# Pacing the last weight conversion, giving the block sums buffers of their own, and dropping a scan buffer in a fused recurrence and two-MLP kernel

## The chip, the cores and the metric

The kernel runs on one core of one Trainium2 chip, alone. The metric is the device time of one execution in microseconds (us); less is better. A profiled execution gives, beside its time, the span from the first to the last instruction.

## The reference

A linear recurrence over 768 steps on 32 heads (4 batches, 8 heads of size 40) is followed by two MLPs over its 3072 tokens of width 320. Everything comes in as float64 words for the MLP weights and float32 for the rest; the output is float32.

```python
for t in range(S):                       # the recurrence, per head
    y[:, :, t] = einsum('bhd,bhde->bhe', rt, state)
    Sa = einsum('bhde,bhe->bhd', state, at)
    state = state * wt[:, :, None, :] - einsum('bhd,bhe->bhde', Sa, bt) + einsum('bhd,bhe->bhde', vt, kt)
...
h = x @ w_in                             # first MLP, 320 -> 2048 -> 320
x = (maximum(h, 0) + alpha * minimum(h, 0)) @ w_out
...
g = x @ w_gate                           # second MLP, 320 -> 1536 -> 320
out = (g * (1 / (1 + exp(-g))) * (x @ w_val)) @ w_out
```

## The kernel before, in words

**Stages.** The tokens are cut into six pieces m of 128 steps by four batches, 512 columns each. For each piece the recurrence is done in chunk form (`preps`, `inverse`, `seq`), its result goes to DRAM as `xd[m]`, and the first MLP takes that piece as its block j = m (`mlp1`), one piece behind the recurrence, so that blocks 0 to 3 and the start of block 4 run beside the recurrence of the next piece. When the recurrence has ended, its memory pools are closed, and the tail begins: the rest of block 4, block 5 (the last), and then the six blocks of the second MLP.

**Numbers in two halves.** Each float32 operand of a product is split into a high part (an ACT cast, `split`, L198) and the rest (a subtraction, L199), and products are made of high and low parts: 8 matmuls for an up product (`up_mm`, L254) and 8 for a down product (`down_mm`, L260 to L266). Weights come as float64, are turned into float32 by integer work on VectorE, an ACT operation and, for every other tile, two on GpSimd (`gated`, L186 to L194), are split, and are kept in DRAM (`wd`) or, for the last tiles, in memory.

**A block of the first MLP.** For each of 16 tiles f of the hidden width: fetch the up weights (`fetch`, L244), up product into `u`, `prelu` (an ACT relu L294, a VectorE operation L295, the split into `gh` and `gl`), and one step behind it the down product, which adds into three sums `d`. Blocks 0 to 4 fetch into a ring of four weight buffers (pool `wp1`, tag `w`); from tile 10 of block 4 on, tiles are fetched into buffers that block 5 uses again ("resident"). At the end of a block the three sums are copied out (L356, L359, L360) and written to DRAM as `x1d[j]` (L357, L361). Their copies `x1o` stand in the two buffers of tag `g`, which `prelu` uses too. `fill_x` loads and splits the x of a block; for `mlp1` it is traced at a priority raised by 1000.

**Order.** Nothing here waits by hand. A scheduler orders each engine's instructions before the run: of those whose operands and buffers are free by its own reckoning it takes the one with the best priority, which is the place in the traced program, raised where the code says so. `tc.issue_after(x)` puts those instructions of its block that stand on x's own engine behind x in that engine's order. A pool that is opened where closed pools lay waits for the last use of each closed pool that it overlaps.

**The tail's other work.** `direct` converts tiles 4 to 11 of the three weight matrices of the second MLP (24 tiles; gate, value and out in turn) straight into memory; `kept` fetches tiles 0 to 3, converted earlier. During block 5, one tile of `direct` is traced at every `CTAIL`-th step; the rest is traced in the first block of the second MLP, three tiles per f. The x of that first block, `xs0`, is traced right behind the x of block 5. In the second MLP, per f: gate product `pg`, value product `pv` (two buffers each), a Silu on ACT (`sg`, L986), a product, a split, and the down products (L972 to L974). The pool `gp` with `sg` is opened when the pools of the first MLP are closed.

**The scan of `prep_a`.** Each item (a batch of a piece) has a scan of the decays (L525) into `rest`, of which two exist; from it come `Wx` (L532) and `AN` (L539) in `prep_a`, and `kbt` in `prep_b` (L552). `preps` traces `kbt` of an item ahead of the scan of the next.

Of the kernel before, what the change touches and what calls it, by code (L numbers as in the profile page):

```python
# [7 lines left out]
F32 = mybir.dt.float32  # L8
F32R = mybir.dt.float32r
U32 = mybir.dt.uint32  # L10
# [8 lines left out]
XPRI = 1000  # L19
# [20 lines left out]
ZB = 2  # L40
# [7 lines left out]
YB = 1  # L48
# [10 lines left out]
GPB = 2  # L59
DEP = 1  # L60
HOLD = 10
CTAIL = 8
XB = 2
L = 64
HALF = 32
LOOK = 2
AHEAD = 3
KEEP = 4

@with_exitstack  # L70
def kernel(
# [15 lines left out]
    nc = tc.nc  # L87
    NM, B, _, D, NP, TB = r.shape
    NT, DM = out.shape
# [3 lines left out]
    NSEG = NP * CPB  # L93
    NG = B * NSEG
    BLK = B * TB
    NB = NT // BLK
    K1 = DFF // 128
    K2 = DFF2 // 128
    RT = DM - 256
    lo, hi = slice(0, 64), slice(64, 128)  # L100
# [4 lines left out]
    x1d = [dram.tile([DM, BLK], F32, name=f"x1d{m}") for m in range(NM)]  # L105
# [49 lines left out]
    mark = {}  # L155

    @contextmanager
    def lifted():
        tc.cur_priority -= XPRI
        yield  # L160
        tc.cur_priority += XPRI

    def words(x):
        return x.bitcast(U32).rearrange("f (n two) -> f n two", two=2)
# [13 lines left out]
    LEAST = 1.125 * 2.0 ** -15  # L178

    def gated(pool, raw, dve=0):  # L180
        whi, wlo = raw[..., 1], raw[..., 0]
        sh = list(whi.shape)
        y = pool.tile(sh, U32, tag="wy", name="wy", bufs=YB)
        z = pool.tile(sh, U32, tag="wz", name="wz", bufs=ZB)
        f = z.bitcast(F32)
        nc.vector.tensor_scalar(y, whi, 0x07FFFFFF, 3, ALU.bitwise_and, ALU.logical_shift_left)  # L186
        nc.vector.scalar_tensor_tensor(z, whi, 0xC0000000, y, ALU.bitwise_and, ALU.bitwise_or)
        nc.vector.scalar_tensor_tensor(y, wlo, 29, z, ALU.logical_shift_right, ALU.bitwise_or)
        nc.scalar.activation(out=f, in_=whi.bitcast(F32), func=ACTF.Abs)
        if dve:  # L190
            nc.vector.scalar_tensor_tensor(f, f, LEAST, y.bitcast(F32), ALU.is_ge, ALU.mult)
            return f
        nc.gpsimd.tensor_scalar(f, f, LEAST, None, ALU.is_ge)
        nc.gpsimd.tensor_tensor(out=f, in0=f, in1=y.bitcast(F32), op=ALU.mult)  # L194
        return f

    def split(raw, h, l, eng):
        nc.scalar.copy(out=h, in_=raw)  # L198
        eng.tensor_tensor(out=l, in0=raw, in1=h.bitcast(F32), op=ALU.subtract)  # L199
# [87 lines left out]
    def load_x(pool, src, n):  # L287
        xs = new_x(pool, n)
        fill_x(pool, xs, src, 0, n)
        return xs  # L290

    def prelu(gpool, ps, f, n):
        g = gpool.tile([128, n], F32, tag="g", name="g")
        nc.scalar.activation(out=g, in_=ps, func=ACTF.Relu, scale=-1.0)  # L294
        nc.vector.scalar_tensor_tensor(g, g, neg[:, f:f + 1], ps, ALU.mult, ALU.add)  # L295
        gh = gpool.tile([128, n], F32R, tag="gh", name="gh")
        gl = gpool.tile([128, n], F32R, tag="gl", name="gl")
        split(g, gh, gl, nc.gpsimd if f % 16 < PGL else nc.vector)
        return gh, gl
# [18 lines left out]
    def mlp1(j, early=0):  # L318
        psd, xp1, gp1, wp1 = (e1p[k] for k in ("psd", "xp", "gp", "wp"))
        fs = [*range(HOLD, K1), *range(HOLD)] if j == NM - 1 else range(K1)  # L320
        half = B // 2 * TB
        xs = new_x(xp1, BLK)
        plan = [(f, 0, half) for f in range(early)] + [(f, half, BLK) for f in range(early)]
        plan += [(f, 0, BLK) for f in fs if f >= early]
        dps = [psd.tile([128, BLK], F32, tag=f"d{q}", name=f"d{q}") for q in range(3)]
        pend = []
        done = ups

        def down(f, c0, c1, gh, gl):
            t = fetch(wp1, 2 * f + 1, False, j, done)  # L330
            for q in range(3):
                down_mm(dps[q][:, c0:c1], q, t, gh, gl, f == fs[0] and c0 == 0, f == fs[-1])

        seen = set()
        for f, c0, c1 in plan:
            if not seen & {(c0, c1), (0, half) if early and c0 == 0 else (c0, c1)}:
                with lifted():
                    b0, b1 = c0 // TB, c1 // TB
                    fill_x(xp1, xs, xd[j][:, b0:b1].rearrange("f b t -> f (b t)"), c0, c1)
                seen.add((c0, c1))  # L340
                yield
            t = fetch(wp1, 2 * f, True, j, done)
            ps = e1p["psu"].tile([128, c1 - c0], F32, tag="u", name="u")
            done.append(up_mm(ps, t, tuple(x[..., c0:c1] for x in xs)))
            yield
            if len(pend) == DEP:
                down(*pend.pop(0))
            pend.append((f, c0, c1, *prelu(gp1, ps, f, c1 - c0)))
            yield
        for e in pend:  # L350
            down(*e)
        for q in range(3):
            tc.cur_priority -= XPRI
            o = gp1.tile([128, BLK], F32, tag="g", name="x1o")
            if q < 2:
                nc.scalar.copy(out=o, in_=dps[q])  # L356
                nc.sync.dma_start(out=x1d[j][q * 128:q * 128 + 128], in_=o)  # L357
            else:
                nc.scalar.copy(out=o[lo], in_=dps[2][hi])  # L359
                nc.vector.tensor_tensor(out=o[lo], in0=dps[2][lo], in1=o[lo], op=ALU.add)  # L360
                mark["x1"] = nc.sync.dma_start(out=x1d[j][256:DM], in_=o[lo])  # L361
            tc.cur_priority += XPRI
            yield
# [21 lines left out]
    nc.gpsimd.memset(first, 0.0)  # L385
    reset = first[:, 0:NSEG // 2]
    nc.gpsimd.memset(reset[:, :, 0:1], 1.0)
    rests = [rawp.tile([128, NSEG, L + 1], F32, name=f"rest{j}") for j in range(2)]
    mask = pers.tile([128, L], F32, name="mask")

    def masks():
# [526 lines left out]
    wg, wv2, w2 = {}, {}, {}  # L918
    KINDS = ((wg, moe2_w_gate, "up"), (wv2, moe2_w_val, "up"), (w2, moe2_w_out, "down2"))

    def direct():
        for f in range(KEEP, K2):
            for j, (held, src, kind) in enumerate(KINDS):
                t = wpool.tile([128, 768 if kind == "up" else 2 * DM], F32R, tag=f"w{j}", name=f"w{j}")
                conv(tail, 2 * K1 + 3 * f + j, src, f, kind, t, (3 * f + j) % 2)
                held[f] = t.rearrange("p (a b) -> p a b", a=6) if kind == "up" else t
                yield

    def kept(f):
        for j, (held, _, kind) in enumerate(KINDS):  # L930
# [6 lines left out]
    with ExitStack() as st:  # L937
        e1p["psu"] = st.enter_context(tc.tile_pool(name="psu3", bufs=3, space=PSUM))
        for _ in gm:
            pass  # L940
        XAB[0] = 4
        gm = mlp1(NM - 1)
        next(gm)
        xs0 = load_x(xp, x1d[0], BLK)
        for k, _ in enumerate(gm):
            if k % CTAIL == 2:
                next(c2, 0)
        last1 = fetched[-2 * HOLD:]
        for f in range(KEEP):
            with tc.issue_after(last1[LOOK + 4 * f].ins):  # L950
                kept(f)
# [100 lines left out]
```

## Time and profile before

| | us |
|---|---|
| median of 3 runs (1256.48 to 1261.86) | 1259.91 |
| the profiled execution's own time | 1257.29 |
| its span | 1255.3 |
| outside the span | 2.0 |
| TensorE (PE) busy in the span | 1100.4 |
| VectorE (DVE) busy | 754.6 |
| ScalarE (ACT) busy | 605.0 |
| GpSimd (POOL) busy | 282.0 |

Times in rows are us from the start of the span, lengths of single instructions in us unless marked ns. PE is TensorE's matmuls, PEld its weight loads, SPq the queue of SyncE, which issues nearly all transfers. A bracket behind a row gives the time that the engine sat idle before it and what ended it. "Clock" is the granted clock of TensorE as a share of 2.4 GHz. The profiled execution lies 2.6 us under the median.

### The profile page before, as it was taken

What the parts mean: (1) busy time and instruction counts of PE and PEld (TensorE: products, weight loads), DVE (VectorE), ACT (ScalarE), POOL (GpSimd) and SP (SyncE); (2) the same over time, 40 slices, a digit from 0 to 9 for tenths busy, and PEclk for the clock granted to TensorE, in tenths of its full rate; (3) what the DMA queues carried; (4) which work ended last, traced back from release to release, by engine and by line L of the source; (5) the groups of instructions that cost most, each with busy time, mean ns of one, the idle gap of its engine ahead of it and who ended that gap; (6) DMA issues with size and microseconds to landing.
All of it is one profiled execution on the core that took longest, in us unless ns stands there. A gap on an engine that the chain in (4) does not pass through costs nothing.

```text
span 1255.3 us, 24461 instructions
## 1 busy us (share of the span) xinstructions
PE 1100.4 (88%) x9056; PEld 936.4 (75%) x9056; DVE 754.6 (60%) x1624; ACT 605.0 (48%) x1495; POOL 282.0 (22%) x452
## 2 busy tenths in 40 slices
PE   4147678999999889998999968897999999999998
PEld 3146567787878768787788746685888888888887
DVE  7898987697599579859684345456632323232222
ACT  5559559646935763855644333344432323232222
POOL 8335434301212211530471022124400000000000
PEclk9668687999999999999999988998999999999999
DMA  5635688566454544735675795423110101000000
GB/s 145 195 118 165 207 281 268 168 193 183 133 164 131 179 129 142 234 110 150 198 258 162 263 352 193 135 76 120 47 47 1 46 1 39 1 21 1 21 1 21
DMA packets 94885, 166.36 MB, mean 133 GB/s; under 512 B 13232, under 2 KB 43184, under 8 KB 94768
## 3 DMA queue, kind: packets, MB, share of 16 engines
q1 hardware_dynamic: 86608, 160.88, 40.8%
q10 hardware_dynamic: 8160, 3.93, 1.1%
q8 instruction: 72, 1.18, 0.4%
q14 instruction: 45, 0.37, 0.1%
HBM read 136.98 MB, written 27.79 MB: 131 GB/s over the span
## 4 chain that ended last, share of the span: by engine, by line
PE 57%; DMA 9%; DVE 8%; ACT 7%; issue 2%; POOL 1%; SPq 1%; ACTq 0%; DVEq 0%; POOLq 0%
PE pg L254 10%; PE pv L254 10%; PE u L254 9%; PE o L973 3%; PE o L972 3%; PE o L974 3%; PE d L260 2%; DMA wt<-wd 2%; PE d L261 2%; PE d L262 2%; PE gp L762 2%; DMA raw<-in_moe_w_gate_dram 2%; PE yp L777 1%; PE mnp L564 1%; DMA xd<-pv 1%
## 5 line engine op out<-in xcount | busy, mean ns | idle before, releaser
L198 ACT CAST gh<-g 128x512 fp32r<-128x512 f32 (+1 forms) x176 | 105.7, 601 | 170.7 <-DVE g L988 115.3
L199 DVE TENSOR_TENSOR gl<-g,gh 128x512 fp32r<-128x512 f32 (+1 forms) x176 | 122.0, 693 | 93.7 <-ACT gh L198 88.9
L988 DVE TENSOR_TENSOR g<-pv,sg 128x512 f32<-128x512 f32 x72 | 49.8, 691 | 208.5 <-PE pv L254 205.2
L254 PE MATMUL u<-xh,wt 128*128 128x512 f32 (+1 forms) x416 | 151.2, 405 | 26.3 <-DVE g L295 14.3
L295 DVE SCALAR_TENSOR_TENSOR g<-g,neg,u 128x512 f32<-128x512 f32 (+1 forms) x104 | 73.0, 703 | 90.9 <-ACT g L294 90.5
L254 PEld LDWEIGHTS u<-xh,wt 128*128 128x128 f32 x416 | 80.7, 198 | 46.5 <-DVE g L295 17.5
L254 PE MATMUL pg<-xh,w 128*128 128x512 f32 x288 | 102.8, 398 | 8.7 <-ACT sg L986 8.7
L986 ACT ACTIVATE sg<-pg 128x512 f32<-128x512 f32 x72 | 42.9, 597 | 128.6 <-PE pg L254 128.6
L294 ACT ACTIVATE g<-u 128x512 f32<-128x512 f32 (+1 forms) x104 | 58.5, 565 | 93.2 <-PE u L254 84.7
L254 PE MATMUL pv<-xh,w 128*128 128x512 f32 x288 | 100.5, 390 | 0.0
L973 PE MATMUL o<-w,gh 128*128 128x320 f32 x288 | 87.8, 309 | 0.0
L972 PE MATMUL o<-w,gh 128*128 128x320 f32 x288 | 87.3, 309 | 0.0
L261 PE MATMUL d<-gl,wt 128*128 128x512 f32 (+1 forms) x208 | 83.1, 401 | 0.3 <-DVE gl L199 0.3
L625 DVE TENSOR_TENSOR tmp<-la 128x96 f32<-128x96 f32 (+43 forms) x306 | 80.5, 287 | 2.2 <-POOL la L613 0.4
L254 PE MATMUL u<-xl,wt 128*128 128x512 f32 (+1 forms) x208 | 81.3, 391 | 0.0
L262 PE MATMUL d<-gh,wt 128*128 128x512 f32 (+1 forms) x208 | 81.0, 391 | 0.0
L720 POOL COPY gs<-raw_v 64x160 f32<-64x160 f32 x96 | 42.2, 439 | 172.5 <-PE yp L777 110.8
L564 PE MATMUL mnp<-AN,kbt 128*128 128x128 f32 x384 | 60.6, 309 | 22.2 <-DVE AN L539 15.6
L633 DVE TENSOR_TENSOR la<-la,tmp 128x96 f32<-128x96 f32 (+43 forms) x306 | 77.8, 280 | 2.0
L260 PE MATMUL d<-gh,wt 128*128 128x512 f32 (+1 forms) x208 | 73.7, 407 | 5.3 <-DMA wt<-wd 4.1
L578 POOL TENSOR_SCALAR_AFFINE_SELECT AN<-AN 64x256 f32<-64x256 f32 x96 | 53.0, 552 | 110.1 <-ACT AN L577 98.1
L974 PE MATMUL o<-w,gl 128*128 128x320 f32 x288 | 76.9, 308 | 0.0
(123 smaller groups left out, 2619.5 us busy)
## 6 DMA issues: line engine op xcount, KB each, us to landing
wt<-wd SPq DMA_DIRECT2D x98, 384.0 KB
wt<-wd SPq DMA_DIRECT2D x98, 320.0 KB
wd<-wc SPq DMA_DIRECT2D x24, 384.0 KB
raw<-in_moe_w_out_dram SPq DMA_DIRECT2D x28, 320.0 KB
raw_bk<-in_bk_dram SPq DMA_DIRECT2D x48, 160.0 KB
wd<-wc SPq DMA_DIRECT2D x20, 320.0 KB
raw<-in_moe_w_in_dram SPq DMA_DIRECT2D x16, 256.0 KB
raw_v<-in_v_dram SPq DMA_DIRECT2D x24, 160.0 KB
```

The costliest lines, as they stand in the source:

```text
L198: nc.scalar.copy(out=h, in_=raw)
L199: eng.tensor_tensor(out=l, in0=raw, in1=h.bitcast(F32), op=ALU.subtract)
L254: last = nc.tensor.matmul(ps, lt, rh, start=(i == 0), stop=(i == len(ops) - 1))
L260: nc.tensor.matmul(ps, wh, gh, start=first, stop=False)
L261: nc.tensor.matmul(ps, wh, gl, start=False, stop=False)
L262: nc.tensor.matmul(ps, wl, gh, start=False, stop=last)
L564: nc.tensor.matmul(ps[:, s].rearrange("p h t -> p (h t)"), kbt[:, g * SH + s].rearrange("p j t -> p (j t)"), an[:, :, g * SH + s, :],)
L625: nc.vector.tensor_tensor(out=tv, in0=ml[:, kk + 1:HALF, kk:kk + 1].to_broadcast([128, nr, ns]), in1=tl[:, kk:kk + 1, c0:c0 + ns].to_broad ...
L633: mark["inv"] = nc.vector.tensor_tensor(out=dst, in0=dst, in1=tv, op=ALU.subtract)
L972: nc.tensor.matmul(ops[q], gh[:, ts], wh, start=first, stop=False)
L973: nc.tensor.matmul(ops[q], gh[:, ts], wl, start=False, stop=False)
L974: nc.tensor.matmul(ops[q], gl[:, ts], wh, start=False, stop=last)
```

## The change

- `CTAIL` is 6 in place of 8: six steps of `direct` are traced in block 5 in place of five.
- `direct` asks for raw weight tiles two ahead (`ask`), into five raw buffers in place of two, and traces the split of a tile one step behind its conversion (`finish`). `gated` has two and three scratch buffers there, in place of one and two.
- The steps of `direct` in block 5, and the load of `xs0`, stand in `tc.issue_after(ups[-1].ins)`, `ups[-1]` being the last matmul of the latest up product. `xs0` is traced at step 30 of block 5, not ahead of it.
- The x of block 5 is lifted by 100 (`NEAR`), not by 1000.
- `x1o` of the first two sums has a tag of its own with two buffers in the x pool (4 KB of a partition); that of the third is a buffer of the weight ring. The tag `g` of the first MLP has one buffer in place of two.
- `rest` has one buffer in place of two (2 KB of a partition).

The diff:

```diff
@@ -59,11 +59,14 @@
 GPB = 2
 DEP = 1
 HOLD = 10
-CTAIL = 8
+CTAIL = 6
 XB = 2
 L = 64
 HALF = 32
 LOOK = 2
+TRB = 5
+LATE = 30
+NEAR = 100
 AHEAD = 3
 KEEP = 4
 
@@ -155,10 +158,10 @@
     mark = {}
 
     @contextmanager
-    def lifted():
-        tc.cur_priority -= XPRI
+    def lifted(n=XPRI):
+        tc.cur_priority -= n
         yield
-        tc.cur_priority += XPRI
+        tc.cur_priority += n
 
     def words(x):
         return x.bitcast(U32).rearrange("f (n two) -> f n two", two=2)
@@ -178,10 +181,11 @@
     LEAST = 1.125 * 2.0 ** -15
 
     def gated(pool, raw, dve=0):
+        yb, zb = (YB, ZB) if pool is stage else (2, 3)
         whi, wlo = raw[..., 1], raw[..., 0]
         sh = list(whi.shape)
-        y = pool.tile(sh, U32, tag="wy", name="wy", bufs=YB)
-        z = pool.tile(sh, U32, tag="wz", name="wz", bufs=ZB)
+        y = pool.tile(sh, U32, tag="wy", name="wy", bufs=yb)
+        z = pool.tile(sh, U32, tag="wz", name="wz", bufs=zb)
         f = z.bitcast(F32)
         nc.vector.tensor_scalar(y, whi, 0x07FFFFFF, 3, ALU.bitwise_and, ALU.logical_shift_left)
         nc.vector.scalar_tensor_tensor(z, whi, 0xC0000000, y, ALU.bitwise_and, ALU.bitwise_or)
@@ -290,7 +294,7 @@
         return xs
 
     def prelu(gpool, ps, f, n):
-        g = gpool.tile([128, n], F32, tag="g", name="g")
+        g = gpool.tile([128, n], F32, tag="g", name="g", bufs=1)
         nc.scalar.activation(out=g, in_=ps, func=ACTF.Relu, scale=-1.0)
         nc.vector.scalar_tensor_tensor(g, g, neg[:, f:f + 1], ps, ALU.mult, ALU.add)
         gh = gpool.tile([128, n], F32R, tag="gh", name="gh")
@@ -334,7 +338,7 @@
         seen = set()
         for f, c0, c1 in plan:
             if not seen & {(c0, c1), (0, half) if early and c0 == 0 else (c0, c1)}:
-                with lifted():
+                with lifted() if j < NM - 1 else lifted(NEAR):
                     b0, b1 = c0 // TB, c1 // TB
                     fill_x(xp1, xs, xd[j][:, b0:b1].rearrange("f b t -> f (b t)"), c0, c1)
                 seen.add((c0, c1))
@@ -351,7 +355,8 @@
             down(*e)
         for q in range(3):
             tc.cur_priority -= XPRI
-            o = gp1.tile([128, BLK], F32, tag="g", name="x1o")
+            o = xp1.tile([128, BLK], F32, tag="xo", name="x1o", bufs=2) if q < 2 else wp1.tile([128, 768], F32, tag="w", name="x1o")
+            o = o[:, 0:BLK]
             if q < 2:
                 nc.scalar.copy(out=o, in_=dps[q])
                 nc.sync.dma_start(out=x1d[j][q * 128:q * 128 + 128], in_=o)
@@ -385,7 +390,7 @@
     nc.gpsimd.memset(first, 0.0)
     reset = first[:, 0:NSEG // 2]
     nc.gpsimd.memset(reset[:, :, 0:1], 1.0)
-    rests = [rawp.tile([128, NSEG, L + 1], F32, name=f"rest{j}") for j in range(2)]
+    rests = [rawp.tile([128, NSEG, L + 1], F32, name="rest")] * 2
     mask = pers.tile([128, L], F32, name="mask")
 
     def masks():
@@ -918,13 +923,45 @@
     wg, wv2, w2 = {}, {}, {}
     KINDS = ((wg, moe2_w_gate, "up"), (wv2, moe2_w_val, "up"), (w2, moe2_w_out, "down2"))
 
+    tiles = [(f, j) for f in range(KEEP, K2) for j in range(3)]
+    raws = {}
+
+    def ask(n):
+        if n < len(tiles):
+            f, j = tiles[n]
+            _, src, kind = KINDS[j]
+            sw = words(src)
+            if kind == "up":
+                raws[n] = tail.tile([128, 3, 128, 2], U32, tag="raw", name="raw", bufs=TRB)
+                sw = sw[:, f * 128:f * 128 + 128]
+                nc.sync.dma_start(out=raws[n][:, 0:2], in_=sw[0:256].rearrange("(j p) n two -> p j n two", p=128))
+                for p in (lo, hi):
+                    nc.sync.dma_start(out=raws[n][p, 2], in_=sw[256:DM])
+            else:
+                raws[n] = tail.tile([128, DM, 2], U32, tag="raw", name="raw", bufs=TRB)
+                nc.sync.dma_start(out=raws[n], in_=sw[f * 128:f * 128 + 128])
+
     def direct():
-        for f in range(KEEP, K2):
-            for j, (held, src, kind) in enumerate(KINDS):
-                t = wpool.tile([128, 768 if kind == "up" else 2 * DM], F32R, tag=f"w{j}", name=f"w{j}")
-                conv(tail, 2 * K1 + 3 * f + j, src, f, kind, t, (3 * f + j) % 2)
-                held[f] = t.rearrange("p (a b) -> p a b", a=6) if kind == "up" else t
-                yield
+        bits = None
+        ask(0)
+        ask(1)
+        for n in range(len(tiles) + 1):
+            ask(n + 2)
+            new = gated(tail, raws.pop(n), n % 2) if n < len(tiles) else None
+            if n:
+                finish(*tiles[n - 1], bits)
+            bits = new
+            yield
+
+    def finish(f, j, w32):
+        held = KINDS[j][0]
+        t = wpool.tile([128, 768 if j < 2 else 2 * DM], F32R, tag=f"w{j}", name=f"w{j}")
+        if j < 2:
+            held[f] = t.rearrange("p (a b) -> p a b", a=6)
+            split(w32, held[f][:, 0:3], held[f][:, 3:6], nc.gpsimd)
+        else:
+            held[f] = t
+            split(w32, t[:, 0:DM], t[:, DM:2 * DM], nc.gpsimd)
 
     def kept(f):
         for j, (held, _, kind) in enumerate(KINDS):
@@ -941,10 +978,13 @@
         XAB[0] = 4
         gm = mlp1(NM - 1)
         next(gm)
-        xs0 = load_x(xp, x1d[0], BLK)
         for k, _ in enumerate(gm):
             if k % CTAIL == 2:
-                next(c2, 0)
+                with tc.issue_after(ups[-1].ins):
+                    next(c2, 0)
+            if k == LATE:
+                with tc.issue_after(ups[-1].ins):
+                    xs0 = load_x(xp, x1d[0], BLK)
         last1 = fetched[-2 * HOLD:]
         for f in range(KEEP):
             with tc.issue_after(last1[LOOK + 4 * f].ins):
```

## Rows read from the trace of the kernel before

**Rows 1.** Stretches: us; busy PE, PEld, DVE, ACT, POOL (instructions); clock, DMA share, GB/s.

```profile
700.00:765.00 65.00, 47.07 (x172) 35.64 (x171) 29.32 (x49) 21.96 (x38) 9.40 (x10) 0.87 0.95 333
765.00:846.00 81.00, 76.86 (x326) 61.97 (x325) 43.74 (x68) 33.63 (x60) 14.39 (x14) 0.98 0.35 106
846.00:870.00 24.00, 15.33 (x60) 11.89 (x60) 15.61 (x26) 10.87 (x19) 9.83 (x9) 0.86 0.45 137
870.00:1250.00 380.00, 379.56 (x1969) 333.84 (x1967) 120.34 (x178) 106.56 (x189) 17.73 (x16) 1.00 0.07 21
702.00:708.00 6.00, 5.44 (x17) 4.35 (x18) 2.78 (x5) 2.66 (x5) 0.00 (x0) 0.72 0.59 171
...
864.00:870.00 6.00, 5.30 (x17) 4.26 (x18) 5.19 (x9) 3.92 (x8) 1.12 (x1) 0.68 0.19 55
```

**Rows 2.** Waits of PE from 700 to 765: total us, times, longest.

```profile
PE u L254 <- DMA wt<-wd: 7.9, 3, 5.5
PE d L260 <- DMA wt<-wd: 2.6, 2, 2.0
```

**Rows 3.** Timeline of 696 to 704: start, length, what, idle before and releaser.

```profile
698.87 0.58 ACT L359 COPY x1o<-d 64x512 f32<-64x512 f32 x1 [1.65 <-DMA x1d<-x1o]
...
701.13 0.60 ACT L294 ACTIVATE g<-u 128x512 f32<-128x512 f32 x1 [1.67 <-DMA x1d<-x1o]
...
702.56 0.50 PE L254 MATMUL u<-xh,wt 128*128 128x512 f32 x1 [2.46 <-DVE g L295]
```

**Rows 4.** Timeline of 791 to 794, the same columns as rows 3.

```profile
791.30 0.58 ACT L359 COPY x1o<-d 64x512 f32<-64x512 f32 x1 [1.67 <-DMA x1d<-x1o]
...
793.35 0.80 PE L254 MATMUL u<-xh,wt 128*128 128x512 f32 x1 [4.14 <-DVE g L295]
```

**Rows 5.** Timeline of 848 to 866, the same columns.

```profile
848.09 0.62 PE L254 MATMUL pg<-xst,w 128*128 128x512 f32 x2
...
860.18 0.47 SPq L361 DMA_DIRECT2D x1d<-x1o  x1
...
862.75 1.28 ACT L986 ACT_TABLE_LOAD   x1 [0.56 <-DMA x1d<-x1o]
...
864.70 0.79 PE L254 MATMUL pg<-xh,w 128*128 128x512 f32 x1 [8.67 <-ACT sg L986]
```

**Rows 6.** Timeline of SyncE's queue, 700 to 815: transfers in order of issue.

```profile
703.70 0.80 SPq L279 DMA_DIRECT2D xa<-xd  x2
...
705.69 11.79 SPq L244 DMA_DIRECT2D wt<-wd  x16
...
735.49 4.78 SPq L244 DMA_DIRECT2D wt<-wd  x6
...
798.66 4.69 SPq L244 DMA_DIRECT2D wt<-wd  x2
```

**Rows 7.** DMA issues by line, 700 to 765: count, size of each.

```profile
xa<-x1d SPq DMA_DIRECT2D x5, 256.0 KB
```

**Rows 8.** Timeline of ScalarE and VectorE around two up products of the tail.

```profile
751.03 0.60 ACT L294 ACTIVATE g<-u 128x512 f32<-128x512 f32 x1 [4.43 <-PE u L254]
...
753.09 0.69 DVE L199 TENSOR_TENSOR gl<-g,gh 128x512 fp32r<-128x512 f32 x1 [0.68 <-ACT gh L198]
...
843.74 0.60 ACT L294 ACTIVATE g<-u 128x512 f32<-128x512 f32 x1
...
847.70 0.68 DVE L199 TENSOR_TENSOR gl<-g,gh 128x512 fp32r<-128x512 f32 x1
```

**Rows 9.** The chain that ended last, 820 to 832: start, us, what.

```profile
826.80 2.04 PE u L254 x9
```

**Rows 10.** Timeline of VectorE, 249 to 296: one item's scan, and a later product.

```profile
249.57 1.27 DVE L525 TENSOR_TENSOR_SCAN rest<-wseg,first 128x260 f32<-128x260 f32 x2
...
254.04 1.21 DVE L539 TENSOR_TENSOR AN<-raw_a,Wx 128x1024 f32<-128x1024 f32 x1
...
294.82 1.22 DVE L552 TENSOR_TENSOR kbt<-raw_bk,rest 128x1024 f32<-128x1024 f32 x1
```

## The prediction

> **What bounds the kernel now.** I read the stretches first, then the waits of TensorE, then the timelines at each large wait. From 870 to 1250 us PE is busy 379.56 of 380 us at full clock [rows 1]: the second MLP's six blocks are bound by PE's own work, nothing in the change makes that work less, and the time can only be won ahead of it. In the tail ahead of it PE is idle 17.9 us of 700 to 765, 4.1 of 765 to 846 and 8.7 of 846 to 870 [rows 1], 30.7 us together. In the first of these stretches the DMA engines are busy 95% at 333 GB/s [rows 1], and most of PE's idle time there is waits for first-MLP weights, 10.5 us in five waits [rows 2]: that stretch is bound by bytes. Three other waits have another cause, and it is the same each time: the end of a block.
>
> At the end of block 3, ACT's copy of the third sum and the next relu both wait until a sum's transfer has landed, because the sums stand in the two `g` buffers; PE then waits 2.46 us for the product of that relu [rows 3]. At the end of block 4 it is the same, 4.14 us [rows 4]. At the end of block 5 the gate product is complete soon after 848.7 and its Silu could run, but ACT starts the table load for it at 862.75, released by the landing of the last sum, whose transfer was issued at 860.18; PE is idle 8.67 us [rows 5]. The pool of `sg` reuses the memory of the pool in which the sums stand.
>
> After such waits the clock is at its lower level for some microseconds: its mean is 0.72 over 702 to 708 and 0.68 over 864 to 870 [rows 1]. A stretch of 6 us at 0.72 loses 6 x 0.28 = 1.7 us, at 0.68 1.9 us, of which 0.2 are within the wait, so 1.7 as well. I take 1.6 for the wait at 793, which lies between these two in length.
>
> **The change, part by part.** The sum is made against the profiled execution: span 1255.3, its own time 1257.29, so 2.0 us lie outside. The median of the runs, 1259.91, is 2.6 above it; I add that at the end.
>
> *End of block 3.* With sums 0 and 1 in `xo` and sum 2 in the weight ring, the relu waits for no transfer. Gain 2.46 + 1.7 = 4.2. It must not be lost again behind it: the tail's fetches have to start earlier too. Now SyncE stands until 703.70 for the x of block 5, which comes ahead of the weights because it is lifted by 1000, and the run of 16 weight fetches starts only at 705.69 [rows 6]. Lifted by 100, the x stands behind block 4's remaining fetches, and the run can start near 701, when the recurrence's pools close. 705.69 less 701 is 4.7, enough to carry the 4.2. Bounds: 0 (the bytes decide) to 4.7.
>
> *The stretch bound by bytes, 700 to 765.* Moved out: `xs0`, and with it the x of the block after, which now follow block 5's fetches in priority. The stretch carries five pieces of 256 KB of them [rows 7], and by the code two more of that size in halves: 1.8 MB, or 5.4 us at 333 GB/s. Moved in: three more raw tiles, since five may be outstanding in place of two; by their shapes (128 x 384 or 128 x 320 words of 8 bytes) at most 1.2 MB, 3.5 us. Every tile of `direct` issues the same transfers as before. I do not count on pacing: `ups[-1]` is a matmul, and the block under `issue_after` traces nothing on PE, so by the rule of that construct nothing is put behind it. The trace agrees: block 5's fetches are traced under the same construct, behind up products of block 5, yet counted along the queue the first of them leaves within the run of six from 735.49, while block 4 is still computed, and only the last five leave from 798.66 on [rows 6]. So the raw tiles run ahead as before. Net -1.9; x data that is ready may still go early, so I take -1. Bounds -5.4 to +3.5.
>
> The Trainium skill ("DMA: Bandwidth & Descriptors", section "Queues, rings and completion order") says that each DMA engine consumes a queue's descriptors in ring order, which speaks against asking ahead on the one SyncE queue: a weight tile asked for behind five raw tiles waits for all their bytes. By that rule alone the term would be +3.5 and not -1. The trace agrees as far as a full queue and waits for weights stand together [rows 1, 2].
>
> *End of block 4.* The same cure: 4.14 + 1.6, less 0.5 for PE waiting on the copies of the sums themselves (ACT's 0.58 for the last [rows 4]). Gain 5.2. Bounds 0 to 5.7.
>
> *End of block 5.* Its sums 0 and 1 now stand in the left x pool and sum 2 in the weight ring; by the sizes, the x pool of blocks 0 to 4 grows to cover all of the new pool `gp`, so that `sg` waits neither for `g` nor for sum 2. Silu can run right after the gate product. PE's wait of 8.67 goes, and 1.7 of clock; I leave 1.3 for the table load of 1.28 [rows 5], which may still stand in front. Gain 9.1. Bounds: 2.7, if `sg` still waits for all three sums and only the chain of copies is shorter, to 10.4.
>
> The skill ("ScalarE: Activation LUTs", section "What ACT_TABLE_LOAD costs") gives 2.66 us for a switch with its drain, and by that 1.4 us less would be gained; no drain stands apart in the trace, so I keep the 1.28 [rows 5].
>
> *One `g` buffer.* The next relu must now wait for the end of the subtraction that reads `g`. From relu to the end of that subtraction it is 751.03 to 753.78, 2.75 us, where nothing else runs, and 843.74 to 848.38, 4.64 us, where conversions and x splits crowd in [rows 8]. A tile of the hidden width costs PE 16 matmuls at 2.04 / 9 = 0.227 [rows 9], 3.63 us. Uncrowded the chain fits; crowded it does not, by 1.0 us. Some 26 tiles are done in the tail. Two `gh` buffers and three `u` buffers take up single delays, so I take +1.5; bounds 0 to 26 x 1.0 = 26. Beside the recurrence `u` has one buffer, and the up product waits for that chain's second step already: nothing.
>
> *One `rest` buffer.* Now the scan of an item runs far ahead: one at 249.57, while a product `kbt` of an item before it comes at 294.82 [rows 10]. With one buffer that scan, and the work to `AN` (to 255.25), must come behind that product. Its own part of the time to 255.25 is the scan, 1.27, `AN`, 1.21 [rows 10], and the scan for `Wx` between, which runs over as many elements as the first: 3.8 us, in four of the pieces, that move from the recurrence's inverse into the stretch of products. VectorE alone takes them there, and PE has the first MLP to go on with. I take +1; bounds 0 to 4 x 3.8 = 15.
>
> *At nothing:* the copies into `xo` in place of `g` (same instructions); a weight buffer held for the third sum (four in the ring, next fetches already out); splits one behind, more scratch and `CTAIL` (24 tiles by the same instructions; PE did not wait for a converted tile after 870 [rows 1]). The split of `xs0` moves into block 5, six operations of 0.6 to 0.7 us on two engines, hidden behind PE at 95% busy and ACT at 42% [rows 1]; uncovered, 4 us. PE will come to the first block some 15 us sooner, and conversion then is the next thing that could be late.
>
> Sum: -4.2 - 1.0 - 5.2 - 9.1 + 1.5 + 1.0 = -17.0. Span 1238.3, that execution 1240.3, with 2.6 for the median 1243.
>
> **The rivals.** A change of 0.5% (6.3 us) is about what a measurement here can tell from none.
>
> *Bytes take it back.* If five raw tiles ahead of the weights cost 3.5 us, and the gain at block 3 (4.2) and at block 4 (5.2) is lost in waiting for weights and converted tiles, the end of block 5 remains: -9.1 + 2.5, or 1253. For it: 95% in the first stretch. Against: DMA at 35% from 765 on [rows 1].
>
> *One scan buffer stretches the recurrence.* All 15 us are paid: -18.0 + 15 gives about 1257, no change. For it: the early scans are real. Against: PE has other work.
>
> *Slower: the chain of one `g` buffer.* If every tile of the tail takes the crowded 4.64 us, +26 stands against -18.5: 1267. It eats the whole gain from 3.63 + 18.5 / 26 = 4.3 us a tile on. For it: the crowded rows. Against: conversions are done in pieces, and most tiles are like the first pair.
>
> *The pacing works after all.* Then the raw tiles leave the first stretch, 1.9 MB as they are now, some 6 us more: 1237. Against it: the construct's rule and the queue.
>
> **How the numbers follow.** The forecast, all ends of blocks cured and the rest small: 0.58, with its own range 1237 to 1250. Bytes take it back: 0.14. Scan buffer: 0.12. Chain of `g`: 0.09. Pacing works: 0.07. Faster takes the first, the last and a part of the bytes case, less some of the forecast's upper edge: 0.68; same 0.20; slower 0.12. The range runs from 1233 (pacing, and all bounds kind) to 1262 (the scan case), and leaves out the chain of `g` and a little at either end.
>
> **What would show it.** In the changed profile: no wait of a relu or a copy for `x1d<-x1o`; PE idle under 1.5 us at the ends of blocks 4 and 5; the first Silu within 3 us of its gate product; the run of weight fetches starting near 701; waits for `wt` near 10 us still. It would be wrong if relus wait for `gl` all through block 5, if the product `kbt` of the recurrence comes later by whole microseconds per piece, if weights are waited for by 15 us and more, or if PE waits for converted tiles in the first block of the second MLP.

## The result, and the profile after

The changed kernel takes 1271.42 us (median of 4 runs, 1270.27 to 1273.06), the kernel before 1260.88 beside it. The ratio is 1.008, 95% interval 1.0052 to 1.0108: slower by 0.8%, where 1243 was forecast. The profiled execution has a span of 1268.5, before 1255.3, so 13.2 us have to be found.

The stretches of the changed kernel, in the columns of [rows 1]:

```profile
700.00:765.00 65.00, 37.73 (x137) 27.86 (x136) 30.20 (x54) 19.23 (x35) 13.80 (x13) 0.76 0.97 350
765.00:846.00 81.00, 80.69 (x343) 64.89 (x342) 39.65 (x60) 33.40 (x57) 9.04 (x8) 0.98 0.44 134
846.00:870.00 24.00, 21.86 (x87) 16.82 (x86) 19.75 (x29) 12.11 (x25) 12.37 (x11) 0.94 0.32 101
870.00:1250.00 380.00, 378.18 (x1948) 331.79 (x1948) 121.26 (x179) 109.43 (x192) 18.29 (x16) 1.00 0.06 20
```

In 700 to 765 the DMA engines move more than before, 350 GB/s in place of 333, and PE does less: 27.3 us idle in place of 17.9, at a mean clock of 0.76 in place of 0.87, 137 matmuls in place of 172 [rows 1]. From 765 to 846 PE hardly stops, 0.3 us in place of 4.1. These fixed stretches hide that the work is at another point in each kernel, so the rest is read from the recurrence's last product to the first gate product: 700.1 to 846.6 before, 701.8 to 866.8 after. Those two rows, before and after, each from its own trace:

```profile
700.10:846.60 146.50, 124.44 (x497) 97.82 (x497) 73.52 (x117) 55.59 (x98) 23.79 (x23) 0.93 0.61 206
```

```profile
701.80:866.80 165.00, 135.29 (x529) 105.64 (x529) 85.75 (x137) 63.55 (x114) 33.22 (x30) 0.90 0.63 213
```

This stretch is 18.5 us longer. Of that, 165.00 - 135.29 = 29.7 us are idle in place of 22.1, so +7.6. There are 32 more matmuls, since the first MLP was two tiles further behind when the recurrence ended: 32 x 0.227 [rows 9] = +7.3. The other 3.6 are put down to PE's busy time at the lower clock (mean 0.90 in place of 0.93). The recurrence itself ends 1.7 later. From the first gate product to the end it is 401.7 in place of 408.7, 7.0 less: the wait of 8.67 for Silu [rows 5] is gone, and a new one of 1.8 for `gl` has come. 18.5 + 1.7 - 7.0 = 13.2, what was to be found.

Most of the idle time is waits for first-MLP weights, 25.2 us in five waits where there were 10.5 [rows 2]. PE's waits from 700 to 765 (total, times, longest):

```profile
PE u L258 <- DMA wt<-wd: 24.3, 4, 8.7
...
PE d L264 <- DMA wt<-wd: 0.9, 1, 0.9
```

SyncE's queue after, in order of issue:

```profile
701.52 0.38 SPq L937 DMA_DIRECT2D raw<-in_moe_w_gate_dram  x1
701.95 1.11 SPq L939 DMA_DIRECT2D raw<-in_moe_w_gate_dram  x2
703.11 0.59 SPq L937 DMA_DIRECT2D raw<-in_moe_w_val_dram  x1
703.74 0.48 SPq L939 DMA_DIRECT2D raw<-in_moe_w_val_dram  x1
707.04 1.77 SPq L248 DMA_DIRECT2D wt<-wd  x4
...
717.23 0.48 SPq L939 DMA_DIRECT2D raw<-in_moe_w_val_dram  x1
717.99 0.34 SPq L942 DMA_DIRECT2D raw<-in_moe_w_out_dram  x1
...
767.38 14.74 SPq L248 DMA_DIRECT2D wt<-wd  x9
```

Two raw tiles, all but one transfer of the second, lead the tail's queue now, ahead of the first weights at 707.04; before, x and then weights led it, from 703.70 and 705.69 [rows 6]. The last of block 4's weights for the ring leaves within the run from 767.38, at 781.81 counted along the queue, 80.0 us after the recurrence's end; before it left at 756.07, 56.0 after.

The ends of blocks are cured. The timeline of ScalarE at the end of block 4, and of PE and ScalarE at the end of block 5:

```profile
811.59 1.08 ACT L361 COPY x1o<-d 128x512 f32<-128x512 f32 x2 [1.26 <-PE d L266]
...
813.21 0.59 ACT L364 COPY x1o<-d 64x512 f32<-64x512 f32 x1
...
813.94 0.60 ACT L298 ACTIVATE g<-u 128x512 f32<-128x512 f32 x1
...
866.76 0.56 PE L258 MATMUL pg<-xh,w 128*128 128x512 f32 x1 [2.07 <-DVE g L299]
...
869.25 1.06 PE L258 MATMUL pg<-xst,w 128*128 128x512 f32 x2
...
870.39 1.28 ACT L1026 ACT_TABLE_LOAD   x1 [2.39 <-PE pg L258]
...
871.68 0.60 ACT L1026 ACTIVATE sg<-pg 128x512 f32<-128x512 f32 x1
```

No copy and no relu waits for a sum's transfer, PE's wait of 4.14 at the end of block 4 [rows 4] is gone, and in place of 8.67 at the end of block 5 [rows 5] PE waits 2.07.

### The profile page after: what moved, and what is told of

Read it like the earlier page. It is cut to its first block, busy times and chain, and to the rows that moved or that the text cites. A ratio compares the mean times of both kernels' runs of the same rounds, so it can differ in the third digit from the quotient of the medians.

```text
span 1268.5 us, 24421 instructions
## 1 busy us (share of the span) xinstructions
PE 1106.8 (87%) x9056; PEld 939.8 (74%) x9056; DVE 752.3 (59%) x1624; ACT 607.1 (48%) x1495; POOL 294.0 (23%) x452
## 4 chain that ended last, share of the span: by engine, by line
PE 56%; DVE 15%; ACT 11%; DMA 8%; issue 6%; POOL 3%; SPq 1%; ACTq 0%; DVEq 0%; POOLq 0%
PE pg L258 10%; PE pv L258 10%; PE u L258 9%; PE o L1014 3%; PE o L1013 3%; PE o L1012 3%; DMA wt<-wd 2%; DVE tmp L630 2%; PE gp L767 2%; DVE la L638 2%; PE d L264 2%; PE yp L782 2%; PE d L265 2%; PE d L266 2%; PE mnp L569 2%
## 5 line engine op out<-in xcount | busy, mean ns | idle before, releaser
L258 PE MATMUL u<-xh,wt 128*128 128x512 f32 (+1 forms) x416 | 156.2, 417 | 35.7 <-DMA wt<-wd 29.1
L258 PEld LDWEIGHTS u<-xh,wt 128*128 128x128 f32 x416 | 83.8, 205 | 58.0 <-issue 14.8
L569 PE MATMUL mnp<-AN,kbt 128*128 128x128 f32 x384 | 60.8, 309 | 27.7 <-DVE AN L544 15.7
L266 PE MATMUL d<-gh,wt 128*128 128x512 f32 (+1 forms) x208 | 80.3, 388 | 0.0
L569 PEld LDWEIGHTS mnp<-AN,kbt 128*128 128x128 f32 x384 | 54.3, 217 | 32.4 <-DVE AN L544 13.6
L203 POOL TENSOR_TENSOR wc<-wz,wc 128x384 fp32r<-128x384 f32 (+3 forms) x60 | 57.4, 968 | 82.1 <-ACT wc L202 72.9
L725 POOL COPY gs<-raw_v 64x160 f32<-64x160 f32 x96 | 46.1, 480 | 128.4 <-PE yp L782 34.9
```

Of the source, the lines that this page charges most:

```text
L258: last = nc.tensor.matmul(ps, lt, rh, start=(i == 0), stop=(i == len(ops) - 1))
L266: nc.tensor.matmul(ps, wl, gh, start=False, stop=last)
L569: nc.tensor.matmul(ps[:, s].rearrange("p h t -> p (h t)"), kbt[:, g * SH + s].rearrange("p j t -> p (j t)"), an[:, :, g * SH + s, :],)
```

## The experiments

The theories are three: *queue*, what SyncE hands out ahead of the weights that block 4 needs next makes the loss; *scan*, the one rest buffer makes it; and, against both, that any reordering of this kernel's queues moves the time as much. All kernels do the whole computation. Ratios are to the kernel before, in 5 rounds, with 95% intervals.

**The parts alone.** One buffer, in the kernel before:

```
-    rests = [rawp.tile(..., name=f"rest{j}") for j in range(2)]
+    rests = [rawp.tile(..., name="rest")] * 2
```

> The kernel before with one rest buffer in place of two, nothing else. Scan theory (one buffer holds back the last scans ahead of the second inverse, where PE has no first MLP yet; in the changed kernel that inverse starts at 124.2 in place of 119.6 and the first MLP stays two tiles behind): slower by 4 to 8 us, 1265 to 1269, with the second inverse starting near 124 and 2 tiles fewer of u at 600 us. Bytes theory (the whole loss arises in 700 to 765 from raw tiles asked ahead): within 2 us of before. My prediction had +1.

1273.46 us, 1.0101 (1.0078 to 1.0123). That is more than expected. The recurrence ends 4.9 us later than in before (705.0), and 546 matmuls are left from there to the first gate product in place of 497.

The new tail without the rest of the change (two `rest`, two `g`, sums in `g`):

> The kernel before with the new tail alone (raw tiles asked two ahead with five buffers, split one behind, CTAIL 6, the x of block 5 lifted by 100, the x of the second MLP later); sums in g, two g and two rest buffers as before. Bytes theory: 5 to 6 more raw tiles of 0.33 to 0.39 MB go in 700 to 765, PE waits for weights 20 us and more there, and the time is 6 to 12 us over before, 1267 to 1272. Scan theory alone: within 3 us of before, since the rest buffers are two.

1280.32, 1.015 (1.0125 to 1.0175). From the end of the recurrence to the first gate product 38.0 us are idle (row below).

The changed kernel with two `rest` buffers, and the kernel before with the sums alone moved:

```
+    o = xp1.tile(..., tag="xo", bufs=1) if q < 1 else wp1.tile([128, 768], ..., tag="w")
     rests = [... for j in range(2)]
```

> The changed kernel with two rest buffers again (to make room, only the first sum has its own buffer, the second and third stand in the weight ring). Scan theory: the second inverse starts near 120 again and the time falls by 4 to 8 us under the changed kernel, 1263 to 1267. Bytes theory alone: as the changed kernel, 1269 to 1273.

1264.69, 1.0027 (1.0006 to 1.0048).

> The kernel before with the sums moved out of g (first sum in its own buffer, the others in the weight ring), one g buffer, two rest buffers, and the tail as before. Theory that the ends of blocks are cured by the sums alone, and the loss is from the scan and from the bytes: faster by 8 to 15 us, 1245 to 1252, with the waits at the ends of blocks 4 and 5 (4.14 and 8.67) under 3 us. Rival, the chain of one g buffer costs as much as the ends give: 1257 to 1264, with relus waiting for gl all through block 5.

1247.29, 0.9891 (0.9865 to 0.9917): the lowest median here, faster than both. The wait at block 4's end is gone, and 0.7 us is left of the 8.67, beside a new 1.6 ahead of the first gate product.

**What the tail costs by.** The raw tiles put behind a transfer, so that the construct binds on SyncE:

```
-    with tc.issue_after(ups[-1].ins):
+    with tc.issue_after(fetched[-1].ins):
```

> The changed kernel with the raw tiles and the first x of the second MLP put behind a transfer of SyncE's own queue (the last weight fetch traced so far) in place of an up product, so that the wait binds. Bytes theory (raw tiles that leave ahead of block 4's weights cost the stretch 700 to 765): no raw tile before the run of weight fetches at 707, waits for weights there fall from 25 to 12 us or less, time 8 to 14 us under the changed kernel, 1257 to 1264. Rival, the bytes only move into later blocks and are waited for there: within 3 us of the changed kernel, with waits for converted tiles or weights after 765.

1270.55, 1.0084 (1.0053 to 1.0116): no gain, the rival's result. The last fetch traced is one of the held weights, which leaves at 718, far ahead of the ring's last (781): 17 raw transfers still went ahead of the ring's last one, in place of 31. Waits for weights fell to 15.7 us, but PE's idle time in the stretch stayed at 28.9, with waits for `g` and `gl` in their place.

> As tail_only, but with three raw buffers in place of five. Theory that the number of raw tiles outstanding sets the loss: 2 tiles (0.7 MB, 2 us at 333 GB/s) and more fall out of 700 to 765, 1268 to 1277, 3 us or more under tail_only. Rival, that the tiles are asked early at all (with CTAIL 6 and the lower lift) makes the loss: 1278 to 1282.

1279.21, 1.0154 (1.0123 to 1.0184) with `TRB = 3`: by the time, the rival's result. The trace says less. With three buffers 21 raw transfers go ahead of the ring's last fetch in place of tail_only's 28, the waits for weights are 17.6 us in place of 26.8, and the stretch to the first gate product is 6.3 shorter (158.9); the recurrence ends 3.3 later, which takes half of that back. The number outstanding is a part of the loss and not the whole.

The tail split in two, the conversion alone and the x loads alone:

```
(tail_direct)  NEAR = 1000, CTAIL = 8, xs0 where it was, direct() and ask() new
(tail_near)    NEAR = 100, LATE = 30, direct() as before
```

> The kernel before with the new conversion alone (raw tiles asked two ahead, five raw buffers, split one behind, two wy and three wz buffers), the x loads lifted and placed as before and CTAIL 8. Theory that the conversion running ahead makes the loss of tail_only (19 us): 1272 to 1280, with waits for weights of 15 us and more between the end of the recurrence and the first gate product. Rival, that the lower lift and the later x make it: within 4 us of before.

1281.26, 1.0156 (1.012 to 1.0192), waits for weights 27.9 us.

> The kernel before with only the x of block 5 lifted by 100 and the first x of the second MLP placed later, the conversion as before. Theory that the conversion makes the loss of tail_only: within 4 us of before, 1258 to 1265. Rival, that lift and place make it: 1270 to 1280.

1264.65, 1.0025 (1.0002 to 1.0048). The conversion makes the loss by itself, 21 us over before; lift and place of the x are 4.5 over it, just clear of the noise.

**The order of the queue.** Now behind block 4's last fetch into the ring (`rings[-1]`, kept where `fetch` draws from the ring):

```
-    with tc.issue_after(ups[-1].ins):            # raw tiles, xs0
+    with tc.issue_after(rings[-1].ins):
...
-    with tc.issue_after(done[-AHEAD].ins) if ... # block 5's weights (hold_behind, *_all_, after2_)
+    with tc.issue_after(rings[-1].ins) if j == NM - 1 else nullcontext():
```

> As tail_only, with all raw tiles and the first x of the second MLP put behind block 4's last fetch into the weight ring on SyncE (4 of block 5's fetches are ahead of it then, and no raw transfer). Queue theory: the loss of tail_only goes, PE's idle time from the end of the recurrence to the first gate product falls from 38.0 us to 22 or less, 1256 to 1264. Rival, the conversion's own work on VectorE and GpSimd, or tiles that are then late, make the loss: 1270 and over.

1261.88, 0.9998 (0.9975 to 1.0022): 18 us under tail_only by the order of one queue.

> The changed kernel with the raw tiles and the first x of the second MLP behind block 4's last fetch into the ring. Queue theory: waits for weights between the recurrence's end and the first gate product fall from 25 us to 10 or less, the time by 8 to 16 us under the changed kernel, 1255 to 1263. Rival, as after_paced the bytes only move: 1267 to 1273, with waits for converted tiles in the second MLP's first block.

1253.68, 0.994 (0.9916 to 0.9963): 18 us under the changed kernel, and faster than before.

> The kernel before with block 5's 20 weight fetches behind block 4's last fetch into the ring (14 of them, 4.9 MB, 15 us at 333 GB/s, are ahead of it in before). Queue theory: the waits for weights of 10.5 us in 700 to 765 fall to 5 or less, 1248 to 1257. Rival, block 5 waits for the same weights instead: 1258 to 1265.

1250.70, 0.9914 (0.9891 to 0.9937): the kernel before had the same fault in small, 11 us of it. The waits for weights fell to 6.2, not to 5 or less.

> As sums_two_rests (1247), with block 5's weights and the raw tiles behind block 4's last fetch into the ring; only 2 of block 5's fetches and 6 raw transfers are ahead of it there. Queue theory: a small gain or none, 1243 to 1249. Rival, tiles converted late: 1250 and over, with waits of PE for converted tiles after 850.

1248.59, 0.9908 (0.9885 to 0.9932): where little stood ahead, nothing is gained.

The stretch from the recurrence's last to the first gate product, in the columns of [rows 1], for tail_only, tail_behind, after_behind, hold_behind and sums_two_rests, each from its own trace:

```profile
702.40:867.60 165.20, 127.21 (x496) 98.02 (x496) 87.73 (x134) 58.62 (x107) 34.76 (x32) 0.91 0.61 203
```

```profile
705.80:847.10 141.30, 118.60 (x491) 93.69 (x492) 84.53 (x130) 57.41 (x105) 35.09 (x31) 0.94 0.70 235
```

```profile
701.10:850.80 149.70, 132.23 (x531) 103.18 (x529) 87.81 (x137) 62.53 (x114) 34.62 (x30) 0.93 0.72 234
```

```profile
703.60:838.70 135.10, 121.31 (x498) 96.15 (x496) 72.05 (x116) 54.99 (x98) 24.96 (x23) 0.95 0.66 224
```

```profile
731.90:850.80 118.90, 110.25 (x466) 87.77 (x465) 69.54 (x111) 51.41 (x93) 24.96 (x23) 0.99 0.73 244
```

Beside them, PE's idle time (length less PE busy), its waits for weights in the stretch, when the ring's last fetch leaves after the recurrence's end, how many of the ring's 20 fetches for block 4 were left then, and the transfers that went ahead of the last one, counted along the queue in the program's order (raw transfers, kept weights of the second MLP, block 5's weights):

```
                 idle  weights  last ring  ring left  raw, kept, block 5's
before           22.1   10.5     +56.0        15      13, 0, 14
after            29.7   25.2     +80.0        20      31, 4, 15
tail_only        38.0   26.8     +69.5        15      28, 4, 15
tail_behind      22.7    3.9     +42.0        15       0, 0, 4
after_behind     17.5    6.7     +57.1        20       0, 0, 4
hold_behind      13.8    6.2     +46.1        15      13, 0, 0
sums_two_rests    8.7    2.7     +34.3        11       6, 0, 2
```

Within a pair that differs in the order alone (tail_only and tail_behind, after and after_behind, before and hold_behind) the idle time falls with what stands ahead: by 15, 12 and 8 us. In the first two pairs the order moves more than raw tiles: 11 of block 5's weights, the kept weights, and nine transfers of the second MLP's x (1.8 MB, ahead of the ring's last fetch in before, after and tail_only alike) go behind too, and no run parts their shares. In sums_two_rests the recurrence ends 31.8 us later than in before, with 11 ring fetches left and few transfers ahead of them: its 14 us are the ends of blocks and a kinder order together, and no run here separates the two. The queue of after_behind:

```profile
719.81 38.74 SPq L250 DMA_DIRECT2D wt<-wd  x22
758.60 0.43 SPq L941 DMA_DIRECT2D raw<-in_moe_w_gate_dram  x1
```

The raw tiles come 57 us later than in the changed kernel, and no wait of PE is put down to a converted tile: over 850 to 920 there are two, 2.0 ahead of the first gate product, which uses a kept tile, and 1.5 for `gl`. The same order also has a price where sums still stand in `g`. The timeline of tail_behind at the end of block 4:

```profile
778.98 0.59 ACT L364 COPY x1o<-d 128x512 f32<-128x512 f32 x1 [1.36 <-PE d L270]
...
784.44 0.54 SPq L365 DMA_DIRECT2D x1d<-x1o  x1
...
788.50 0.58 ACT L367 COPY x1o<-d 64x512 f32<-64x512 f32 x1 [6.23 <-DMA x1d<-x1o]
...
791.26 0.80 PE L262 MATMUL u<-xh,wt 128*128 128x512 f32 x1 [11.67 <-DVE g L303]
```

The first sum's transfer leaves 4.9 us after its copy ended, behind x and raw tiles, and the wait of 4.14 [rows 4] has become 11.67.

**The buffers, and the spread of orders.** The last two runs of the `rest` buffer restrict the single one to the first eight items, or to the others:

```
-    rest = rests[i % 2]
+    rest = rests[i % 2 if i >= 2 * B else 0]     # early; late has i < 2 * B
```

> The kernel before with one rest buffer for the first eight items (the first two inverses) and two from then on. Theory that the loss of one buffer arises ahead of the second inverse, where PE has no first MLP: the second inverse starts near 124 and the time is 7 to 12 us over before, 1268 to 1273, as one_rest_alone. Rival, that the loss arises in the later pieces (scans held back beside the first MLP): within 3 us of before.

1257.80, 0.9968 (0.9947 to 0.999): faster, though the second inverse starts at 122.7 in place of 119.6. The scan theory as I had put it falls: that inverse comes late, and nothing is lost.

> The kernel before with two rest buffers for the first eight items and one from then on, the mirror of rest_one_early (which was 4 us under before, so that the loss of 12 us does not lie ahead of the second inverse). Theory that the loss arises beside the first MLP: 8 to 14 us over before, 1269 to 1275, with PE's idle time over 300 to 500 near 23 us as in one_rest_alone (13.1 in before). Rival, that the loss of one_rest_alone is one order of the queues among many and not the buffer: within 4 us of before.

1264.88, 1.0028 (1.0005 to 1.0051), and PE's idle time over 300 to 500 is 14.5, not 23. The two halves do not add up to the 12 us of the whole. Two controls, with nothing changed but the interleaving (`FAC = 0.98`, `FAC = 1.02`):

> Control: the kernel before with the one constant by which the recurrence's preparation is interleaved with the rest at 0.98 in place of 1.0, which changes the order of the queues and nothing else. If a reordering is worth little by itself: within 3 us of before. If orders alone spread the time as far as the single edits did: 5 us or more to either side, and then a difference of that size is no sign of the edit's mechanism.

1272.17, 1.0095 (1.006 to 1.0129).

> Second control: the kernel before with the interleaving constant at 1.02. Orders spread the time (nudge_098 was 12 us over before): 1262 to 1275 if the order of before is the better end of a spread, 1250 to 1258 if it is the middle of one.

1261.14, 0.9998 (0.9977 to 1.002). The first control loses as much as one_rest_alone, but not in the same way. The stretch from its recurrence's last product to its first gate product:

```profile
716.60:863.50 146.90, 125.02 (x499) 98.09 (x498) 73.35 (x117) 56.05 (x100) 25.82 (x23) 0.93 0.63 211
```

It is as long as before's 146.50 with the same PE time: the loss is that the recurrence ends 16.5 us later, and I found no single wait that explains it. The backlog of the first MLP does not come by reordering: 499 and 497 matmuls are left in the two controls. The tail's runs are not of this kind: in tail_only the recurrence ends 2.3 us later, and the loss lies in the stretch.

> The changed kernel with two rest buffers (first sum in its own buffer, the others in the weight ring), and raw tiles, first x of the second MLP and block 5's weights behind block 4's last fetch into the ring. If the rest buffer still costs what it did (6.7 us in after_two_rests against the changed kernel): 1243 to 1249. If the queue's order was the whole loss: 1250 to 1256, as after_behind.

1258.07, 0.9983 (0.9962 to 1.0003): 4 us over after_behind, where the second `rest` buffer had gained 6.7 in after_two_rests. Both runs also move a sum into the weight ring, and after2_behind block 5's weights, so neither difference says what the buffer costs.

> The kernel before with all three sums in the weight ring and the two g buffers kept, two rest buffers, the tail as before. Theory that one g buffer costs some us beside the recurrence (waits of u for g 8.7 us over 130 to 300 in sums_two_rests, 2.9 in before): 1240 to 1245, under sums_two_rests. Rival, that the third ring buffer held for a sum costs as much: 1246 to 1252.

1260.37, 0.9999 (0.9976 to 1.0022). All sums in the ring, two `g`: the ends of blocks are cured as well (1.0 us left at block 5's end), but waits for weights are 15.5 us. That one `g` buffer costs anything was not seen. Why the waits for weights are 13 us more than in sums_two_rests stays open; the third sum's place in the ring is one candidate.

## Why the prediction was wrong

**The step that failed: the stretch bound by bytes, taken at -1.** Its bound on the other side, 3.5 us, counted three raw tiles more in flight. But five buffers bound what is in flight at once, not what passes while a weight waits. The tiles are converted and asked for again sooner, and at the head of the queue each takes the place of a weight that PE needs next: 31 raw transfers (13 tiles) and 4 kept weights go ahead of the ring's last fetch in place of 13 (5 tiles) and 0, and that fetch leaves 24 us later after the recurrence's end. With one more of block 5's weights that is 4.9 MB more by the shapes, at 333 GB/s an estimate of 15 us. What the runs showed in place of -1 is +18 to +21: in the trace of the changed kernel 14.7 us more of waiting for weights and 3.6 at the lower clock, and 21 us for the new conversion alone (tail_direct against before). The pair after and after_behind, 17.7 us, shows that the order makes it; it is not the term itself, since after_behind also puts behind what before had ahead.

In the profile before I had read the full queue (95%) and the weight waits, and summed the bytes in flight; I did not ask in what order the one queue hands them out. "So the raw tiles run ahead as before" was the sentence that hid it. My rival "bytes take it back" named the mechanism and priced it at 3.5, and its 1253 leaves even those out (with them 1257). Of the signs of being wrong that I had listed, this one came: weights were waited for by 25.2 us. The rule that I set beside the term (the Trainium skill, "DMA: Bandwidth & Descriptors", section "Queues, rings and completion order": each DMA engine consumes descriptors in ring order) pointed the right way, and the pairs above agree with it: 18 us, twice, for the order alone.

**End of block 3, -4.2: not gained.** No relu waits for a landing there any more, but PE waits 6.5 us for a weight right behind it (until 725.83). The run of weights was to start near 701; it starts at 707.04. One part is a wait that I had misread. SyncE stands for the landing of `xd<-pv`, the recurrence's last store, ahead of the x of block 5 in before, and ahead of the weights in after and after_behind. SyncE's waits for it from 700 to 716, in that order, each from its own trace:

```profile
SPq L279 <- DMA xd<-pv: 2.7, 1, 2.7
SPq L248 <- DMA xd<-pv: 2.6, 2, 1.7
SPq L250 <- DMA xd<-pv: 8.2, 1, 8.2
```

With no raw tile ahead (after_behind) the weights start at 704.45, 3.4 after the recurrence's end, so 701 was not to be had. With raw tiles ahead, from 701.52 to 704.22, they start 5.2 after it. The x lifted less did move behind the first weights (708.85), as read; what moved up in its place were raw tiles.

**End of block 4, -5.2: right.** 0.3 us idle in 765 to 846.

**End of block 5, -9.1: right in kind, smaller.** The wait fell from 8.67 to 2.07, by 6.6; the 2.07 is a wait for VectorE's `g` of the last tile. Silu comes within 1.4 us of the gate product, the table load still in front.

**One `g` buffer, +1.5: nothing of it was seen on PE.** From 812 to 868 relus wait for `gl` 9 times, 4.7 us on ScalarE; PE's idle time there is the 2.07 above and 0.3:

```profile
ACT g L298 <- DVE gl L203: 4.7, 9, 0.8
```

**One `rest` buffer, +1: open.** The `kbt` of [rows 10] comes at 295.5 in place of 294.82; the first one of a piece comes 2.6 later in the third piece and 2.5 earlier in the sixth, so no delay adds up per piece. Yet the first MLP is two tiles behind at the recurrence's end in the changed kernel, 7.3 us of the 13.2. That backlog goes with the buffer: 529 matmuls are left with the sums moved and one `rest`, 466 with the sums moved and two (after_two_rests, sums_two_rests), 546 and 497 in the same pair with the sums in `g` (one_rest_alone and before), and the controls and both halves stay at 493 to 499. But the recurrence's end does not follow the backlog: it is 701.8 with one and 727.7 and 731.9 with two where the sums are moved, 705.0 with one and 700.1 with two where they are not. So the backlog alone is not the price. The runs put the price anywhere from -4 to +12, and a control without any buffer changed spans 0 to +12. What the buffer costs in time is not settled.

**Pacing: right that it binds nothing.** `ups[-1]` holds back nothing on SyncE: raw tiles leave at 701.52, 16 us before block 3's sums are copied. What I drew from it, that they run ahead "as before", was wrong: with the next two asked first and five buffers they run further ahead.

## What to carry to other kernels

Where one queue feeds everything, as here, a prefetch is priced by the bytes that leave ahead of the transfer that is waited for next, not by those in flight at once: list what is handed out ahead of that transfer, and put the rest behind it. A wait only paces if it is on the engine that issues; and the anchor has to be the transfer that is late, not the last one written down. Before a difference of 10 us is put down to a buffer, one run that only reorders the queues shows how much of it an order alone can make; here that was 12 us.

## What was not expected

A change of one interleaving constant by 2%, with the same instructions, moved the time by 12 us one way (0.98) and by nothing the other way (1.02).

The table load of ScalarE shows no drain, even where ScalarE comes to it straight from other work. The timeline of sums_two_rests:

```profile
858.37 0.58 ACT L360 COPY x1o<-d 64x512 f32<-64x512 f32 x1
...
858.98 1.28 ACT L987 ACT_TABLE_LOAD   x1
...
860.27 0.60 ACT L987 ACTIVATE sg<-pg 128x512 f32<-128x512 f32 x1
```

The copy ends at 858.95, the load takes 1.28 and Silu starts at 860.27, 1.32 us in all. The Trainium skill ("ScalarE: Activation LUTs", section "What ACT_TABLE_LOAD costs") gives 2.66 us for a switch with its drain; the measurement decides, and here a switch cost half of it.
